# Feed-forward layer over pairs of batches: seven block products in place of eight, with block sums on GpSimd

## The chip, the cores and the metric

The kernel runs on one core of a Trainium2 chip. The core has five engines that run side by side, each with its own queue of instructions in program order: TensorE (PE; its loading of weights is shown apart as PEld), VectorE (DVE), ScalarE (ACT), GpSimd (POOL), and SyncE (SP), which here only issues DMA transfers. The metric is the device time of one execution in microseconds (us). Unchanged, it was 1137.98 us (median of 3 runs, 1137.89 to 1138.92).

## The reference

Attention with a sigmoid in place of the softmax, and then a feed-forward layer with an exact GELU:

```python
scores = (q @ k.T) / np.sqrt(64) - np.log(448)     # 8 batches, 12 heads, 448 positions, 64 wide
x = sigmoid(scores) @ v                            # gathered to 3584 rows of 768
h = x @ w_in                                       # 768 -> 2048
g = 0.5 * h * (1.0 + erf(h / np.sqrt(2.0)))
out = g @ w_out                                    # 2048 -> 768
```

The inputs q, k, v are float32; w_in and w_out are float64.

## The kernel before

**Attention.** A loop over 24 units (a batch and four heads each) runs on PE with sigmoids on ACT. Its output x, laid out with features on partitions, goes to the DRAM scratch `scr_x` from GpSimd's queue. The float64 weights come in as 64-bit integers. `Decoder` turns a chunk of them (16 of 768 columns for w_in, 24 of 512 for w_out) into float32 by five DVE instructions (lines 99 to 124) and two on ACT (110, 113), and GpSimd's queue stores the result in `scr_in` or `scr_out`. 22 of the 40 chunks are decoded beside attention, the other 18 at the start of the feed-forward part (`dec.to`).

**Feed-forward.** `feed_forward` walks over 7 tiles of T = 512 columns of x. In `ffn1` each of the 16 feature blocks of h takes one weight unit and 6 blocks of 128 input features; in `ffn2` each of the 6 output blocks takes two units with 8 blocks of g each. Every product is in split precision: an operand is rounded to a high part (`fp32r`) and the rest is kept as a low part, and three matmuls (low weights by high data, high by low, high by high) are summed in PSUM. So a tile has 16·6·3 + 6·16·3 = 576 matmuls of 512 columns.

**What feeds them.** `Weights.get` keeps three units loaded (`wst`, from scratch by SP, line 173) and four split (`whl`). A split is one cast on ACT for the high part (line 184) and one subtraction on DVE for the low part (line 185). x is loaded and split once for a tile (lines 200 to 207), and g is made by two GELUs on ACT and one subtraction on DVE (413 to 415). Outputs are copied from PSUM by ACT (450) and stored by SP.

**What sets the order.** Each engine runs its instructions in the order in which the code writes them; `ctx.enter_context(tc.manual_schedule())` has no scheduler change it. Buffers rotate, and an instruction that writes a buffer waits for its last reader.

Of the kernel before, what the change touches and what calls it, by code (L numbers as in the profile page):

```python
# [8 lines left out]
F32 = mybir.dt.float32  # L9
# [7 lines left out]
P = 128  # L17
# [4 lines left out]
def tile_sigmoid_attention_gelu_ffn(  # L22
# [19 lines left out]
    T = 512  # L42
    NT = B * S // T
    assert NT * T == B * S and TAIL == D
# [3 lines left out]
    def psum(name, bufs):  # L48
# [7 lines left out]
    xh = const.tile([P, NPAIR, T], F32R, name="xh")  # L56
    xl = const.tile([P, NPAIR, T], F32R, name="xl")

    scr_in = tc.dram_tile([NF, P, NC * P], F32, name="scr_in")
    scr_out = tc.dram_tile([NO, P, NFH * P], F32, name="scr_out")  # L60
    scr_x = tc.dram_tile([P, NPAIR, B * S], F32, name="scr_x")
    WU = max(NC, NFH) * P
    SUB_IN, SUB_OUT = NC * P, NFH * P // 2
    SUB = max(SUB_IN, SUB_OUT)
    WHL, WST = 4, 3
    UNITS = [("in", u) for u in range(NF)] + [("out", u) for u in range(NO)]
    CHUNKS = [
        (kind, u, c0, sub)
        for kind, u in UNITS
        for n, sub in ((NC * P, SUB_IN) if kind == "in" else (NFH * P, SUB_OUT),)  # L70
        for c0 in range(0, n, sub)
    ]

    def width(kind):
        return (NC if kind == "in" else NFH) * P

    def scratch(kind, u):
        return (scr_in if kind == "in" else scr_out)[u]

    class Decoder:  # L80
        def __init__(self):
            self.raws, self.parts, self.done, self.out = {}, {}, 0, None
            self.steps = self.work()
            self.taken = 0

        def load(self, i):
            if i < len(CHUNKS):
                kind, u, c0, w = CHUNKS[i]
                src = (w_in if kind == "in" else w_out)[u].rearrange("p a b -> p (a b)")
                raw = sb.tile([P, 2 * SUB], U32, tag="raw", name=f"raw{i}", bufs=3)[:, : 2 * w]  # L90
# [24 lines left out]
        def end(self, i):  # L115
            kind, u, c0, w = CHUNKS[i]
# [5 lines left out]
            if c0 == 0:  # L122
                self.out = sb.tile([P, WU], F32, tag="wd", name=f"wd_{kind}{u}", bufs=2)
            nc.vector.scalar_tensor_tensor(  # L124
                self.out[:, c0 : c0 + w], m, 2.0**-31, e.bitcast(F32), op0=ALU.mult, op1=ALU.mult
            )
            if c0 + w == width(kind):
                nc.gpsimd.dma_start(scratch(kind, u), self.out[:, : width(kind)])
                self.done += 1

# [20 lines left out]
        def units(self, n):  # L151
# [7 lines left out]
    class Weights:  # L159
# [336 lines left out]
```

## Time and profile before

| | |
|---|---|
| runs | 1137.98 us (1137.89 to 1138.92, n = 3) |
| profiled execution | 1137.48 us, span 1135.7 us |
| attention, on PE | 0 to 255.03 us |
| feed-forward, first to last matmul | 255.03 to 1131.7 us |
| matmuls in the feed-forward part | 4032, of 512 columns each |
| matmuls in attention | 8 of 512 columns to warm up, 1332 of 448 |
| instructions on GpSimd | 56, 52 of them DMA issues |

The span runs from the first instruction to the last; the execution's own time has 1.8 us more around it. The profile page gives the busy time of each engine, the chain of work that ended last, and groups of instructions by line with their mean duration and the idle time ahead of them. The windows give the same by stretches of time, the timeline single instructions. A matmul's shown duration includes its pipeline, so successive ones overlap: their rate is read from the distance of their starts.

### The profile page before, as it was taken

Reading aid. Unit: us, or ns where it says so; the run is one execution under the profiler, and the core shown is the slowest. Engines: PE = TensorE matmul, PEld = TensorE weight load, DVE = VectorE, ACT = ScalarE, POOL = GpSimd, SP = SyncE. Lnnn points to the kernel's source line nnn. Section 1 sums busy time; section 2 is a strip of 40 time slices with the busy share of each in tenths; the row PEclk is TensorE's granted clock in tenths of the full one; section 3 lists DMA queues with packets and bytes.
Section 4 is the critical chain, followed back from the end, with each engine's and each line's share of the span. In section 5 each row is a group of like instructions: output and inputs, shape, how many; then the busy total and the mean of one; then the engine's idle time right before and its main releaser. Section 6 shows DMA issues by size and latency. Waiting matters only on the chain.

```text
span 1135.7 us, 14635 instructions
## 1 busy us (share of the span) xinstructions
PE 1126.3 (99%) x5858; PEld 892.6 (79%) x5858; DVE 536.2 (47%) x646; ACT 544.7 (48%) x749; POOL 37.6 (3%) x56
## 2 busy tenths in 40 slices
PE   9999999999998999999999999999999999999998
PEld 5545555548887888888888888888888888888887
DVE  3777777658987244314433344324432343324420
ACT  5887787776645244324432344324432443334420
POOL 0111111000000000000000000000000000000000
PEclk9999999999999999999999999999999999999999
DMA  9999998868677334433353333533343335433330
GB/s 276 315 308 301 294 301 278 254 220 253 217 267 272 115 108 133 172 93 121 116 172 111 116 106 121 177 113 109 126 167 116 107 111 176 125 102 101 127 121 28
DMA packets 71444, 194.42 MB, mean 171 GB/s; under 512 B 6992, under 2 KB 19920, under 8 KB 71376
## 3 DMA queue, kind: packets, MB, share of 16 engines
q1 hardware_dynamic: 65376, 169.53, 48.0%
q0 software_dynamic: 5696, 23.60, 5.2%
q8 instruction: 46, 0.75, 0.3%
q10 hardware_dynamic: 304, 0.36, 0.1%
q14 instruction: 22, 0.18, 0.0%
HBM read 158.86 MB, written 34.60 MB: 170 GB/s over the span
## 4 chain that ended last, share of the span: by engine, by line
PE 96%; DVE 2%; ACT 1%; issue 0%; ACTq 0%
PE ph L408 13%; PE ph L409 13%; PE ph L410 13%; PE po L436 12%; PE po L438 12%; PE po L437 12%; PE pav L321 10%; PE sc L283 8%; PE sc_t L300 2%; PE pav L334 2%; DVE me L119 1%; DVE whl L185 1%; DVE wd_out L124 0%; ACT me L110 0%; ACT whl L184 0%; PE warm L361 0%
## 5 line engine op out<-in xcount | busy, mean ns | idle before, releaser
L185 DVE TENSOR_TENSOR whl<-wst,whl 128x768 fp32r<-128x768 f32 (+1 forms) x196 | 209.8, 1072 | 285.5 <-ACT whl L184 283.4
L436 PE MATMUL po<-g,whl 128*128 128x512 f32 x672 | 255.5, 380 | 4.0 <-DVE whl L185 4.0
L438 PE MATMUL po<-g,whl 128*128 128x512 f32 x672 | 255.5, 380 | 0.0
L437 PE MATMUL po<-g,whl 128*128 128x512 f32 x672 | 255.3, 380 | 0.0
L408 PE MATMUL ph<-xh,whl 128*128 128x512 f32 x672 | 254.8, 379 | 0.0
L409 PE MATMUL ph<-xl,whl 128*128 128x512 f32 x672 | 254.7, 379 | 0.0
L410 PE MATMUL ph<-xh,whl 128*128 128x512 f32 x672 | 254.7, 379 | 0.0
L184 ACT CAST whl<-wst 128x768 fp32r<-128x768 f32 (+1 forms) x196 | 181.3, 925 | 123.1 <-PE po L438 113.3
L415 DVE TENSOR_TENSOR g<-gf,g 128x512 fp32r<-128x512 f32 x112 | 77.4, 691 | 208.4 <-ACT g L414 208.3
L413 ACT ACTIVATE gf<-ph 128x512 f32<-128x512 f32 x112 | 66.9, 597 | 208.6 <-PE ph L410 183.4
L266 ACT ACTIVATE a<-sc 128x896 f32<-128x896 f32 x144 | 121.8, 920 | 53.4 <-PE sc L283 53.4
L436 PEld LDWEIGHTS po<-g,whl 128*128 128x128 f32 x672 | 127.4, 190 | 22.9 <-DVE whl L185 4.8
L437 PEld LDWEIGHTS po<-g,whl 128*128 128x128 f32 x672 | 127.4, 190 | 18.2
L408 PEld LDWEIGHTS ph<-xh,whl 128*128 128x128 f32 x672 | 127.0, 189 | 18.7 <-DVE whl L185 0.7
L438 PEld LDWEIGHTS po<-g,whl 128*128 128x128 f32 x672 | 127.3, 189 | 18.2
L410 PEld LDWEIGHTS ph<-xh,whl 128*128 128x128 f32 x672 | 127.0, 189 | 18.1
L409 PEld LDWEIGHTS ph<-xl,whl 128*128 128x128 f32 x672 | 127.0, 189 | 18.0
L321 PE MATMUL pav<-a,v 128*64 128x448 f32 x576 | 119.1, 548 | 0.0
L450 ACT COPY ob<-po 128x512 f32<-128x512 f32 x41 | 24.0, 585 | 161.2 <-PE po L438 161.2
L321 PEld LDWEIGHTS pav<-a,v 128*64 128x64 f32 x576 | 37.0, 136 | 68.0 <-issue 63.6
L414 ACT ACTIVATE g<-ph 128x512 fp32r<-128x512 f32 x112 | 66.2, 591 | 0.0
L347 DVE COPY x<-pav 128x448 f32<-128x448 f32 x48 | 29.9, 624 | 62.1 <-PE pav L321 40.4
(43 smaller groups left out, 700.9 us busy)
## 6 DMA issues: line engine op xcount, KB each, us to landing
wst<-scr_in SPq DMA_DIRECT2D x112, 384.0 KB, 3.2
wst<-scr_out SPq DMA_DIRECT2D x84, 512.0 KB, 3.4
v<-v_dram SPq DMA_DIRECT2D x24, 512.0 KB, 5.3
raw<-w_in_dram SPq DMA_DIRECT2D x16, 768.0 KB, 8.3
raw<-w_out_dram SPq DMA_DIRECT2D x24, 512.0 KB, 4.8
scr_x<-x POOLq DMA_DIRECT2D x24, 448.0 KB, 7.0
xl<-scr_x SPq DMA_DIRECT2D x7, 1536.0 KB, 7.8
out_dram<-ob SPq DMA_DIRECT2D x41, 256.0 KB, 2.1
```

The lines of the kernel that those rows point to most:

```text
L184: nc.scalar.copy(hl[:, 0, :w], t[:, :w])
L185: nc.vector.tensor_tensor(hl[:, 1, :w], t[:, :w], hl[:, 0, :w], op=ALU.subtract)
L266: nc.scalar.activation(to, sc, AF.Sigmoid, bias=NEG_LOG_S, scale=SCALE)
L283: nc.tensor.matmul(sc[:, j], ks[rows(j), 1, keys], braid(qs[rows(j), 0]) if braided else qs[rows(j), 0], start=n == 0, stop=n == last,)
L321: nc.tensor.matmul(pav[rows(j)], vals[u][:, p, j, c], a[:, j], start=p == 0 and c == 0, stop=p == 1 and c == FULL - 1,)
L408: nc.tensor.matmul(ph, wl, braid(xh[:, cc]), start=cc == 0, stop=False)
L409: nc.tensor.matmul(ph, wh, braid(xl[:, cc]), start=False, stop=False)
L410: nc.tensor.matmul(ph, wh, braid(xh[:, cc]), start=False, stop=cc == NC - 1)
L415: nc.vector.tensor_tensor(gt[:, 1], gf, gt[:, 0], op=ALU.subtract)
L436: nc.tensor.matmul(po, wl, braid(g[fc][:, 0]), start=fc == 0, stop=False)
L437: nc.tensor.matmul(po, wh, braid(g[fc][:, 1]), start=False, stop=False)
L438: nc.tensor.matmul(po, wh, braid(g[fc][:, 0]), start=False, stop=fc == NF - 1)
```

## The change

**Blocks.** The unit of the feed-forward part is now a pair of batches (4 pairs, b = 0 to 3). Its 896 columns are two blocks (k = 0, 1) of 448, each half of one batch and half of the other. The weights and data are seen as 2 by 2 blocks, and a product of two such matrices is made from seven block products (the Strassen-Winograd scheme) in place of eight. Only the first matrix of the first pair is done plainly (`ffn1_plain`).

**Counts.** The plain one has 16·2·6·3 = 576 matmuls of 448 columns; each of the other seven has 7·72 = 504 (in the first matrix 8 blocks by 3 by 3 terms, in the second 4 steps by 3 by 2 by 3). That is 576 + 7·504 = 4104 matmuls of 448 columns.

**Sums of blocks.** Weights: for each group of four blocks, `mix` makes four sums on GpSimd, and seven DMAs (w_in) or fourteen (w_out) from its queue store the seven operands. For w_out there are 6 groups, formed during `ffn1_plain` as the decoder finishes them; for w_in there are 8, formed in `remix` from the plain scratch `scr_f` during the first pair's second matrix. Data: `x_sum` makes four sums of x on GpSimd for the next pair; `difference_g` (line 501) and lines 672, 674, 675 make sums of g there, 16 of 128x896 for a pair. Results: sums of products stay in PSUM where a chain can be accumulated, else DVE adds them (lines 589 to 595, 652 to 664).

**Splits.** g is kept in float32 and is split when it is used, by `build` (one cast on ACT and one subtraction on DVE of 128x896), two steps ahead, in a ring of three. An operand of x is split by `x_split` (128x1344). A weight unit is 768 wide throughout, 212 of them in place of 196.

```diff
-    T = 512
-    NT = B * S // T
+    NB = B // 2
+    KC, KF, KE = NC // 2, NF // 2, NE // 2
+    IN_ORDER = [
+        (p, s - lag)
+        for chain in ((1, 2), (6, 7, 4), (5, 3))
+        for s in range(KF + len(chain) - 1)
+        for lag, p in enumerate(chain)
+        if 0 <= s - lag < KF
+    ]
+    OUT_ORDER = [(p, c) for p in (1, 2, 5, 6, 3, 7, 4) for c in range(KF // 2)]
...
+    def mix(a, s):
+        a11, a12, a21, a22 = (a[:, i] for i in range(4))
+        s1, s2, s3, s4 = (s[:, i] for i in range(4))
+        nc.gpsimd.tensor_tensor(s1, a21, a22, op=ALU.add)
+        nc.gpsimd.tensor_tensor(s2, s1, a11, op=ALU.subtract)
+        nc.gpsimd.tensor_tensor(s3, a11, a21, op=ALU.subtract)
+        nc.gpsimd.tensor_tensor(s4, a12, s2, op=ALU.subtract)
+        return {1: a11, 2: a12, 3: s4, 4: a22, 5: s1, 6: s2, 7: s3}
...
+        def flush(self):
+            while self.pool and self.pending:
+                (c, e), a = self.pending.pop(0)
+                s = self.pool.tile([P, 4, QUAD], F32, tag="s", name=f"s{c}_{e}", bufs=1)
+                parts = mix(a.rearrange("p (q n) -> p q n", q=4), s)
+                for p in (1, 2, 5, 6, 3, 7, 4):
+                    src = parts[p].rearrange("p (h f n) -> p h f n", h=2, f=2)
+                    for h in range(2):
+                        nc.gpsimd.dma_start(scr_out[p, 2 * c + h][:, :, e], src[:, h])
...
+    def terms(bank, w, op, first, last, chain=False):
+        wh, wl = w
+        hi, lo = op
+        for n, (a, m) in enumerate(((wl, hi), (wh, lo), (wh, hi))):
+            flags = dict(start=first and n == 0, stop=last and n == 2, skip_group_check=chain)
+            nc.tensor.matmul(bank, a, braid(m), **flags)
...
+        def ffn1_plain(g):
...
+            for f in range(NF):
+                if f >= lead:
+                    step(f, 0)
+                step(f, 1)
+                W.prepare_to(f + 1 + WHL)
+                dec.to(AHEAD + 1.5 * (f + 1))
...
+        def ffn1(b, g, ops):
...
+            for n, (p, j) in enumerate(IN_ORDER):
+                if n % 2 == 0:
+                    hl = W.get()
...
+                if (p, j) == (1, 2):
+                    x_split(ops, b, 6)
+                after = {(1, KF - 1): 7, (2, KF - 1): 4, (6, KF - 1): 5, (7, KF - 1): 3}
+                if (p, j) in after:
+                    x_split(ops, b, after[p, j])
...
+            for n, (p, c) in enumerate(OUT_ORDER):
+                hl = W.get()
+                build(n + 2)
...
+                if ahead[0] == 5:
+                    t1, g22 = g[0, 1][ahead[1]], g[1, 1][ahead[1]]
+                    nc.gpsimd.tensor_tensor(t1, g22, t1, op=sub)
+                if p == 6:
+                    nc.gpsimd.tensor_tensor(g11, t2, g11, op=sub)
+                    nc.gpsimd.tensor_tensor(g21, g21, t2, op=sub)
+                if b == 0 and n % 3 == 2 and n // 3 < KF:
+                    remix(n // 3)
...
+        def remix(j):
+            a = sb.tile([P, 4 * QUAD], F32, tag="wd", name=f"a{j}", bufs=2)[:, : 2 * WU]
+            for i in range(2):
+                nc.sync.dma_start(a[:, i * WU : (i + 1) * WU], scr_f[i * KF + j])
+            s = ff.tile([P, 4, QUAD], F32, tag="s", name=f"sin{j}", bufs=1)[:, :, :OP]
+            parts = mix(a.rearrange("p (q n) -> p q n", q=4), s)
+            for p, part in parts.items():
+                n = IN_ORDER.index((p, j))
+                nc.gpsimd.dma_start(scr_in[n // 2][:, n % 2], part)
```

Three places show how the order on an engine changes. The first is PE in the first matrix. Before, in `ffn1`, the rows of one feature block (`ph_6`) are followed by those of the next, each into its own bank, three terms in turn:

```order
L408 MATMUL ph_6_5594<-xh,whl_5508 128x512
L409 MATMUL ph_6_5594<-xl,whl_5508 128x512
L410 MATMUL ph_6_5594<-xh,whl_5508 128x512
L408 MATMUL ph_7_5623<-xh,whl_5537 128x512
L409 MATMUL ph_7_5623<-xl,whl_5537 128x512
L410 MATMUL ph_7_5623<-xh,whl_5537 128x512
```

Now, in the second pair's `ffn1` (`pf` a PSUM bank, `xh_p` and `xl_p` the split operand of a block product), PE alternates between the products of a chain:

```order
L472 MATMUL pf_4819<-xh_p_4757,whl_4777 128x448 x2
L472 MATMUL pf_4819<-xl_p_4758,whl_4777 128x448
L472 MATMUL pf_4819<-xh_p_4757,whl_4777 128x448
L472 MATMUL pf_4875<-xh_p_4721,whl_4777 128x448
L472 MATMUL pf_4875<-xl_p_4722,whl_4777 128x448
L472 MATMUL pf_4875<-xh_p_4721,whl_4777 128x448 x2
```

A matmul has 448 columns for 512, one weight unit serves two products, and a bank is returned to by a second product after others have gone to other banks.

The second place is GpSimd. Before, its queue in the feed-forward part holds only the stores of decoded weights, and it ends with them:

```order
L128 DMA scr_out<-wd_out_3292 128x1024
L128 DMA scr_out<-wd_out_3343 128x1024
L128 DMA scr_out<-wd_out_3398 128x1024
L128 DMA scr_out<-wd_out_3448 128x1024
L492 UNCONDITIONAL_BRANCH
```

Now, in the first pair's second matrix, it holds this (`a` four loaded blocks of w_in, `sin` their sums, `g_01`, `g_11` blocks of g):

```order
L703 DMA scr_in_77<-sin_4123 128x384
L703 DMA scr_in_79<-sin_4123 128x384
L672 TENSOR_TENSOR g_01_3_2772<-g_11_3_2780,g_01_3_2772 128x896
L91 TENSOR_TENSOR sin_4220<-a_4217 128x384
L92 TENSOR_TENSOR sin_4220<-sin_4220,a_4217 128x384
L93 TENSOR_TENSOR sin_4220<-a_4217 128x384
L94 TENSOR_TENSOR sin_4220<-a_4217,sin_4220 128x384
L703 DMA scr_in_70<-a_4217 128x384
L703 DMA scr_in_72<-a_4217 128x384
```

Sums of weights, their stores and sums of g stand in one queue, in the order of the code.

The third place is DVE in the second matrix. Before, in the third tile, there is one subtraction for a weight unit of 1024 and, at the tile's middle, two for x:

```order
L185 TENSOR_TENSOR whl_5169<-wst_5109,whl_5169 128x1024
L207 TENSOR_TENSOR xl<-xl,xh 128x1536 x2
L185 TENSOR_TENSOR whl_5202<-wst_5139,whl_5202 128x1024
L185 TENSOR_TENSOR whl_5235<-wst_5172,whl_5235 128x1024
L185 TENSOR_TENSOR whl_5264<-wst_5205,whl_5264 128x1024
```

Now, in the first pair (`op` the split operand of a step, `tmp` an output, `y` a kept product):

```order
L234 TENSOR_TENSOR whl_4461<-wst_4397,whl_4461 128x768
L263 TENSOR_TENSOR op_21_4466<-g_00_1_2766,op_21_4466 128x896
L660 TENSOR_TENSOR tmp_4475<-pf_4098,y_2_3817 128x448
L660 TENSOR_TENSOR tmp_4484<-pf_4099,y_2_3817 128x448
L660 TENSOR_TENSOR tmp_4493<-pf_4100,y_2_3817 128x448
L234 TENSOR_TENSOR whl_4496<-wst_4438,whl_4496 128x768
L263 TENSOR_TENSOR op_22_4501<-g_00_2_2767,op_22_4501 128x896
```

Each step of 18 matmuls has two subtractions, one for the weights and one for the data, and after a chain's last step the additions that end it.

More of the change, by code (lines that the diff above doesn't have):

```diff
@@ L67, in tile_sigmoid_attention_gelu_ffn @@
[L67 to L71, printed above, removed]
-    ]
[L74 to L78, printed above, removed]
+    WU = NC * P
+    QUAD = KF // 2 * P
+    RAW = 2 * max(WU, 2 * S)
+    WHL, WST = 4, 3
+    IN_ORDER = [
[5 more added lines that the diff above has]
+    ]
@@ new lines, in tile_sigmoid_attention_gelu_ffn @@
+    OUT_ORDER = [(p, c) for p in (1, 2, 5, 6, 3, 7, 4) for c in range(KF // 2)]
+    OP = KC * P
+    assert OP * 2 == WU and KE * P * 2 == WU
+    scr_x = tc.dram_tile([P, NPAIR, B * S], F32, name="scr_x")
+    scr_f = tc.dram_tile([NF, P, WU], F32, name="scr_f")
+    scr_in = [tc.dram_tile([P, 2, OP], F32, name=f"scr_in{i}") for i in range(len(IN_ORDER) // 2)]
+    scr_out = {
+        pc: tc.dram_tile([P, 2, KE, P], F32, name=f"scr_out{pc[0]}_{pc[1]}") for pc in OUT_ORDER
+    }
+    CHUNKS = [("in", u, 0, WU, 0, 0) for u in range(NF)] + [
+        ("out", 2 * ee + h, c * QUAD, QUAD, ij, (c, e))
+        for c in range(2)
+        for e in range(KE)
+        for ij, (ee, h) in enumerate(((e, 0), (e, 1), (e + KE, 0), (e + KE, 1)))
+    ]
@@ L149, in to, with until @@
                 self.taken += 1
-        def units(self, n):
-            while self.done < min(n, len(UNITS)):
+        def until(self, units, groups):
+            while self.done < units or self.groups < groups:
                 next(self.steps)
@@ L244, in load_v, with split_qk @@
             vals[u] = vr
-        def split(u, p):
+        def split_qk(u, p):
             if u >= total:
@@ L374, in attention @@
                 values(u - 1, 0)
[L375 to L376 removed]
+            split_qk(u + 1, 0)
+            split_qk(u + 1, 1)
             for c in range(FULL):
@@ L389, in attention @@
             if u == total - 2:
-                load_x(0)
+                for j in range(2):
+                    x0.append((x_tile("xs", f"xh0_{j}"), x_tile("xs", f"xl0_{j}")))
+                    load_x(x0[j][1], 0, j, 0)
                 W.load_to(2)
             if u == total - 1:
-                split_x()
+                for hi, lo in x0:
+                    split(hi, lo, lo.bitcast(F32))
                 W.prepare_to(2)
```

359 lines of the change are left out of this document (257 added, 102 removed).

## The prediction

> **What bounds the kernel now.** I read the page's busy times first, then windows of the feed-forward part, then the waits. The busy times:
>
> ```profile
> span 1135.7 us, 14635 instructions
> PE 1126.3 (99%) x5858; PEld 892.6 (79%) x5858; DVE 536.2 (47%) x646; ACT 544.7 (48%) x749; POOL 37.6 (3%) x56
> ```
>
> A busy PE is not a PE at its peak, so the rate has to be seen. The windows (length, then busy time and count of PE, PEld, DVE, ACT and POOL, granted clock, DMA share, GB/s) show the start of the feed-forward part, the stretch after it, and the steady one:
>
> ```profile
> 255.00:340.00 85.00, 85.00 (x396) 74.43 (x395) 75.17 (x110) 50.46 (x81) 5.41 (x8) 1.00 0.75 244
> 340.00:400.00 60.00, 56.03 (x251) 48.15 (x250) 32.70 (x40) 24.95 (x34) 1.94 (x3) 0.97 0.57 193
> 400.00:1100.00 700.00, 700.00 (x3245) 612.98 (x3244) 251.26 (x262) 266.22 (x386) 0.00 (x0) 1.00 0.40 126
> ```
>
> In 700 us 3245 matmuls start: 215.7 ns for one of 512 columns, at full clock and without a gap. DVE and ACT are at 36% and 38% there. So in the feed-forward part PE's columns are the bound, except near 340 to 400 us, where PE loses 4.0 us. The waits (who waits for whom, us in total, times, longest) name the cause:
>
> ```profile
> PE po L436 <- DVE whl L185: 4.0, 2, 3.7
> ```
>
> A low part of a weight came late, behind decoding: DVE is busy 75 of the 85 us before.
>
> **What the change removes and adds on PE.** Away go 4032 matmuls: 4032·0.2157 = 869.7 us. In come 4104 of 448 columns. Attention has such matmuls, with half the rows, in pairs on the two halves of the array (PE timeline: start, duration, what, count):
>
> ```profile
> 202.38 0.46 PE L283 MATMUL sc<-lo,hi 64*128 64x448 f32 x2
> 202.68 0.35 PE L283 MATMUL sc<-hi,lo 64*128 64x448 f32 x2
> ...
> 204.00 0.35 PE L283 MATMUL sc<-hi 64*128 64x448 f32 x2
> ```
>
> From 202.68 to 204.00 there are seven starts: 188.6 ns each, which is 215.7·448/512 = 188.7 as well. 4104·0.1886 = 774.0 us. **PE's gain is 95.7 us.** The first row shows what a weight load costs when nothing covers it: 0.30 us to the next start in place of 0.19, so 0.11 us, less than a matmul of 0.19 that runs over it. I therefore take 188.6 ns though each matmul still brings its own load; the load's recorded duration (below, rival 3) is the other end.
>
> The old stall goes: 4.0 us, and the clock of 0.97 over 60 us beside it, 1.8 us. Against the profiled execution (1137.5 us; span 1135.7 and 1.8 around it; the median of the runs, 1138.0, is 0.5 above) a PE that never waits gives 1137.5 − 95.7 − 5.8 = **1036.0 us**. Attention, its decoding and the 8 warming matmuls stay; the tail (a DVE addition in place of ACT's and DVE's copies, and a store) I cost at nothing.
>
> **ACT and DVE.** Their prices, from the groups by shape (count, busy us, mean ns, idle before):
>
> ```profile
> L185 DVE TENSOR_TENSOR whl<-wst,whl 128x768 fp32r<-128x768 f32 x112 | 107.1, 957 | 101.5 <-ACT whl L184 99.4
> L184 ACT CAST whl<-wst 128x768 fp32r<-128x768 f32 x112 | 93.2, 833 | 47.7 <-PE po L438 42.5 <-DMA wst<-scr_in 5.2
> L184 ACT CAST whl<-wst 128x1024 fp32r<-128x1024 f32 x84 | 88.1, 1048 | 75.4 <-PE po L438 70.8 <-DMA wst<-scr_out 4.6
> L258 DVE TENSOR_TENSOR lo<-qk,hi 128x896 fp32r<-128x896 f32 x47 | 51.0, 1085 | 4.3 <-ACT hi L255 2.6 <-DMA v<-v_dram 0.8
> L347 DVE COPY x<-pav 128x448 f32<-128x448 f32 x48 | 29.9, 624 | 62.1 <-PE pav L321 40.4 <-PE pav L334 21.6
> L207 DVE TENSOR_TENSOR xl<-xl,xh 128x1536 fp32r<-128x1536 f32 x14 | 24.0, 1755 | 0.8
> L206 ACT CAST xh<-xl 128x1536 fp32r<-128x1536 f32 x14 | 20.0, 1474 | 0.0
> L255 ACT CAST hi<-qk 128x896 fp32r<-128x896 f32 x21 | 19.9, 950 | 0.0
> L413 ACT ACTIVATE gf<-ph 128x512 f32<-128x512 f32 x112 | 66.9, 597 | 208.6 <-PE ph L410 183.4 <-issue 25.2
> ```
>
> A matrix of seven products takes PE 504·0.1886 = 95.1 us. *Second matrix:* DVE has 28 weight and 28 data subtractions and two of x (1344 wide, 1.56 us by the slope of its rows), 28·(0.957 + 1.085) + 3.1 = 60.3 us, and 15 additions from PSUM of about 0.62, together 70 us. ACT has 28·(0.833 + 0.950) + 2·1.31 + 9·0.54 (a GELU's 0.597 cut to 448) = 57 us. *First matrix:* DVE 28·0.957 + 40·0.62 + 5·1.56 = 59, ACT 23 + 40·0.54 + 5·1.31 = 51. *Plain first matrix* (576·0.1886 = 108.6 us): DVE has 18 chunks of decoding at 3.3 us,
>
> ```profile
> L103 DVE SCALAR_TENSOR_TENSOR me<-raw,me 128x512 uint32<-128x512 uint32 x24 | 19.2, 800 | 0.8
> L119 DVE SCALAR_TENSOR_TENSOR me<-raw,me 128x512 uint32<-128x512 uint32 x24 | 19.1, 797 | 0.2
> L124 DVE SCALAR_TENSOR_TENSOR wd_out<-me 128x512 f32<-128x512 uint32 x24 | 16.6, 692 | 0.8
> L100 DVE TENSOR_SCALAR me<-raw 128x512 uint32<-128x512 uint32 x24 | 11.8, 491 | 0.0
> L99 DVE TENSOR_SCALAR me<-raw 128x512 uint32<-128x512 uint32 x24 | 11.5, 479 | 0.0
> ```
>
> 58.7 us, 16 weight units (15.3) and two of x (3.1): 77 us. All of it fits beside PE if nothing else holds DVE; weights are split three steps ahead (10 us) and data two (6.8 us).
>
> **GpSimd.** No row shows GpSimd computing. Bounds for a sum of two 128x896 blocks: the same work on DVE, 1.09 us; or two passes of an engine that reads one operand at a time, as ACT's cast does, 2·0.950 = 1.90. I take the upper end, because GpSimd's lanes must fetch two operands and the ACT row is the nearest with one operand at a time; both ends stay in the range. By the same doubling 384 wide costs 1.02, 512 wide 1.27, 1344 wide 2.62. GPSIMD Engine Reference of the Trainium skill (3.1, Elementwise, side-by-side cycle accounting) has 4497 ns for a sum of 2048 float32, by proportion an estimated 1.97 us for 896; no run here shows it yet, and the sums below would be some 4% larger. Issues from its queue (timeline) and the time to landing (DMA issues) are there:
>
> ```profile
> 36.57 0.79 POOL L128 DMA_DIRECT2D scr_in<-wd_in  x1 [1.11 <-DVE wd_in L124]
> 188.84 0.71 POOL L350 DMA_DIRECT2D scr_x<-x  x1 [7.62 <-DVE x L347]
> 190.70 0.57 POOL L128 DMA_DIRECT2D scr_in<-wd_in  x1 [1.15 <-DVE wd_in L124]
> wst<-scr_in SPq DMA_DIRECT2D x112, 384.0 KB, 3.2
> scr_in<-wd_in POOLq DMA_DIRECT2D x16, 384.0 KB, 6.8
> ```
>
> At 0.71 for an issue, the plain matrix gives GpSimd 24 sums of 512, 4 of 896 and 84 issues: 38 + 60 = 98 us of 108.6. **The first pair's second matrix** gives it 32 sums of 384, 12 of 896, 4 of 1344 and 56 issues: 33 + 23 + 10 + 40 = 106 us of 95.1. That is too much. Its first remix starts after three steps (10 us); all but the last x sum are ahead of the eighth remix's end, so that ends at 10 + 103 = 113, has landed at 120, is loaded at 123 and split at 125 (0.83 + 0.96). PE wants this data, product (1, 7), 14th of 56 in the next matrix at 1.70 us each: 95.1 + 13·1.70 = 117.2. So 8 us late on GpSimd's own time. A later pair has 23 + 10 = 33 us of sums here, which are hidden.
>
> **Taking turns.** DVE and GpSimd do get in each other's way. The GpSimd issue of 36.57 ended at 37.36, the one of 190.70 at 191.27, while DVE ran
>
> ```profile
> 36.65 0.59 DVE L100 TENSOR_SCALAR me<-raw 128x768 uint32<-128x768 uint32 x1
> 37.27 0.97 DVE L103 SCALAR_TENSOR_TENSOR me<-raw,me 128x768 uint32<-128x768 uint32 x1
> 190.65 0.43 DVE L100 TENSOR_SCALAR me<-raw 128x512 uint32<-128x512 uint32 x1
> ```
>
> The first issue is longer, and ends 0.12 us after DVE's L100; L103, with two operands, then runs over its end. So single-operand DVE work holds an issue up. Whether a GpSimd sum and a two-operand DVE subtraction hold each other up, no row shows: nothing below, a full turn of the other above. I take half a DVE subtraction, met as often as DVE is busy with one: 60.3/95.1 = 0.63, times 0.51 us, times the 47 sums ahead = 15 us, all on the late data. Elsewhere the lead of splits hides most: 2 us for each later second matrix, where eight sums of 896 follow each other (lines 674, 675), 3 for the plain matrix, 2 for the seams. With the 8: 23 + 6 + 3 + 2 = 34 us. **Forecast: 1036.0 + 34 = 1070 us.**
>
> **Rivals.** *1. GpSimd's sums cost nothing to PE*: a sum is priced as on DVE. The second matrix then has 18 + 13 + 6 + 40 = 77 us, done before PE wants it; 1036 plus a few us for seams and tail, 1042. For it speaks that DVE and ACT have 25 to 40 us of slack in every matrix; against it, the price at its lowest.
>
> *2. Full turns*: each GpSimd sum blocks DVE's two-operand work for its whole time and the reverse. In the first pair's second matrix 60 us of DVE and 66 of sums share 95 us; each of 47 sums waits some 0.5 us more, so the data is 33 late in place of 23. In a later one eight sums of 1.9 let one subtraction through each: a step that needs two then takes 2·(1.9 + 1.02) = 5.8 us in place of 3.4 for four steps, and the four sums before them take up the lead: 10 us in each of three. With 6 for the plain matrix, where decoding slows as well, and 2: 71 us, 1107. Page SBUF — State Buffer of the Trainium skill (Who interferes with whom, and the reading of its diagram) states such a lock: exclusive, for the whole instruction, also for DVE with two SBUF inputs against a GpSimd instruction that reads SBUF. The 0.12 us above agrees for issues; the sums are untested here. By that rule the time is this rival's.
>
> *3. The load of weights sets the rate.*
>
> ```profile
> L408 PEld LDWEIGHTS ph<-xh,whl 128*128 128x128 f32 x672 | 127.0, 189 | 18.7 <-DVE whl L185 0.7
> ```
>
> 189 ns is all of a 448-column matmul. If the next could start only some 4 ns after the load's end, 4104·0.004 = 17 us more: 1087. Against it: the 0.11 us above.
>
> *4. Slower than before: GpSimd is the bound of the first pair.* There the time is linear in the price of a sum. Its 104 us of sums and 100 us of issues in the first two matrices already use the time; each tenth on the price is 10 us late at product (1, 7). The 102 us gained are gone when a sum costs 1.75 times my value (over 3.3 us for 896): 34 + 0.75·104 = 112. At twice, 1036 + 34 + 104 = 1174. Nothing in the profile gives such a price.
>
> **How the numbers follow.** Forecast 0.45 (1055 to 1090), rival 1 0.25, rival 2 0.18, rival 3 0.04, rival 4 0.08. The range of 1038 to 1112 leaves out rival 4, and some of the edges of rivals 1 and 2. Faster by over 0.2% (2.3 us, about what a measurement of this kernel can tell from no change) 0.91; within 0.02; slower 0.07.
>
> **What would show it.** Starts of matmuls 188.6 ns apart in a later pair (rival 3: over 192). A wait of PE, through SP's load of `wst`, for a store from GpSimd's queue, in the first 25 us of the second pair's first matrix, some 23 us long (none: rival 1). The mean of GpSimd's 128x896 sums: 1.1 or 1.9 us. In later second matrices PE's waits for DVE at the steps that follow product 5: about 2 us (10: rival 2). I am wrong if PE stalls in first matrices of later pairs, where GpSimd has 8 us of sums.

## The result: 3.4% slower, and the profile after

The changed kernel takes 1177.05 us (median of 4 runs, 1176.37 to 1178.78), the kernel before 1138.10 us in the same comparison (4 runs). The ratio is 1.0343, with a 95% interval of 1.0325 to 1.0361. Forecast were 1070 us, with a range up to 1112.

The page of the changed kernel, with the two lines that answer to those of before:

```profile
span 1175.2 us, 15595 instructions
PE 1071.8 (91%) x5930; PEld 924.2 (79%) x5930; DVE 838.6 (71%) x852; ACT 607.3 (52%) x810; POOL 400.8 (34%) x316
```

PE is no longer busy all the time, though it has less to do. Windows of its eight matrices, from the first matmul of each to that of the next (length, busy time and count of PE, PEld, DVE, ACT and POOL, granted clock, DMA share, GB/s). I call them 1a (the plain first matrix of the first pair), 1b (its second matrix), 2a, 2b and so on to 4b:

```profile
256.07:385.94 129.87, 111.95 (x577) 109.78 (x577) 96.69 (x112) 52.94 (x89) 104.50 (x112) 0.94 0.65 211
385.94:517.62 131.68, 105.85 (x505) 101.43 (x505) 108.84 (x68) 51.12 (x65) 103.10 (x94) 0.87 0.69 239
517.62:628.77 111.15, 99.51 (x505) 97.15 (x505) 69.11 (x80) 51.33 (x76) 23.13 (x17) 0.97 0.41 131
628.77:740.94 112.17, 102.40 (x505) 98.50 (x506) 94.29 (x71) 52.47 (x66) 47.07 (x17) 0.95 0.43 138
740.94:844.79 103.85, 96.24 (x506) 94.83 (x504) 60.29 (x76) 50.72 (x75) 7.09 (x4) 1.00 0.37 117
844.79:959.44 114.65, 104.90 (x505) 100.51 (x505) 94.08 (x71) 52.44 (x66) 47.04 (x17) 0.93 0.42 135
959.44:1063.29 103.85, 96.25 (x506) 94.83 (x504) 60.30 (x76) 50.69 (x75) 7.09 (x4) 1.00 0.37 117
1063.29:1171.00 107.71, 101.17 (x504) 98.07 (x504) 80.39 (x67) 47.63 (x61) 32.95 (x13) 0.95 0.32 101
```

Forecast were 108.6 us for the plain one and 95.1 for the others, plus 34 in all. Each is longer, the two of the first pair most: 21 and 37 us. The last columns show a loss that the forecast did not have at all: the granted clock falls to 0.87 in 1b, and over the span it is 0.961 on average (0.998 before). It is halved in 15 stretches of 92.7 us in all. In 32.6 us of them PE has no matmul and loses nothing by it; in the other 60.1 us it works at half speed. So about 30 us go to the clock.

Two views point at a cause: PE's waits, and the groups of DVE and GpSimd (count, busy us, mean ns, idle before):

```profile
PE pf L472 <- DVE op L263: 49.5, 24, 12.8
PE pf L472 <- ACT op L262: 25.2, 5, 13.9
...
L234 DVE TENSOR_TENSOR whl<-wst,whl 128x768 fp32r<-128x768 f32 x212 | 282.1, 1332 | 182.0 <-ACT whl L233 181.8
L263 DVE TENSOR_TENSOR op<-g,op 128x896 fp32r<-128x896 f32 x112 | 184.5, 1651 | 4.7 <-ACT op L262 4.7
L675 POOL TENSOR_TENSOR g<-g,g 128x896 f32<-128x896 f32 x16 | 43.0, 2688 | 0.0
L674 POOL TENSOR_TENSOR g<-g,g 128x896 f32<-128x896 f32 x16 | 42.5, 2658 | 0.0
L672 POOL TENSOR_TENSOR g<-g,g 128x896 f32<-128x896 f32 x16 | 34.1, 2137 | 97.1 <-DVE op L263 97.0
L595 DVE TENSOR_TENSOR tmp<-pf,g 128x448 f32<-128x448 f32 x72 | 42.4, 616 | 10.3 <-PE pf L472 10.3
```

The same subtraction of 128x768 took 957 ns before and takes 1332 on average here; that of 128x896 went from 1085 to 1651. The addition that reads one operand from PSUM (line 595) is at its expected 0.62 us. The sums of lines 674 and 675, where DVE subtracts all the time, take over 0.5 us more than those of line 672. The timeline (start, duration, and the idle time ahead in brackets) shows it happen, first GpSimd, then DVE, then PE, in 1b:

```profile
458.66 2.10 POOL L674 TENSOR_TENSOR g<-g,g 128x896 f32<-128x896 f32 x1
460.70 2.08 POOL L675 TENSOR_TENSOR g<-g,g 128x896 f32<-128x896 f32 x1
...
468.81 2.06 POOL L675 TENSOR_TENSOR g<-g,g 128x896 f32<-128x896 f32 x1
470.84 1.70 POOL L91 TENSOR_TENSOR sin<-a 128x384 f32<-128x384 f32 x1
...
457.42 14.27 DVE L234 TENSOR_TENSOR whl<-wst,whl 128x768 fp32r<-128x768 f32 x1
471.62 1.88 DVE L263 TENSOR_TENSOR op<-g,op 128x896 fp32r<-128x896 f32 x1
...
473.55 4.75 PE L472 MATMUL pf<-op,whl 128*128 128x448 f32 x15 [12.79 <-DVE op L263]
```

One subtraction lasts 14.27 us: six sums of GpSimd run from 458.66 to 470.87 without a gap, and it ends only when they have. PE then stands for 12.8 us (13.1 from start to start; gaps are given so below). In 2b the two engines alternate instead, and each instruction lasts as long as both together:

```profile
672.73 2.95 POOL L675 TENSOR_TENSOR g<-g,g 128x896 f32<-128x896 f32 x1
675.65 2.80 POOL L674 TENSOR_TENSOR g<-g,g 128x896 f32<-128x896 f32 x1
...
673.64 2.86 DVE L234 TENSOR_TENSOR whl<-wst,whl 128x768 fp32r<-128x768 f32 x1
676.43 2.97 DVE L263 TENSOR_TENSOR op<-g,op 128x896 fp32r<-128x896 f32 x1
```

That suggests, and does not yet show, that the two exclude each other. Three theories were put to the test. **T1**: GpSimd's sums and DVE's subtractions exclude each other, and the stalls cost PE's clock as well. **T2**: GpSimd's own queue takes too long, so data is late. **T3**: the new order has seams of its own (casts behind each other on ACT, splits that are issued late), whatever engine makes the sums.

### The profile page after: what moved, and what is told of

It reads as the page before. It is cut to its first block, busy times and chain, and to the rows that moved or that the text cites. A ratio compares the mean times of both kernels' runs of the same rounds, so it can differ in the third digit from the quotient of the medians.

```text
span 1175.2 us, 15595 instructions
## 1 busy us (share of the span) xinstructions
PE 1071.8 (91%) x5930; PEld 924.2 (79%) x5930; DVE 838.6 (71%) x852; ACT 607.3 (52%) x810; POOL 400.8 (34%) x316
## 5 line engine op out<-in xcount | busy, mean ns | idle before, releaser
L472 PE MATMUL pf<-op,whl 128*128 128x448 f32 x2016 | 415.2, 369 | 76.8 <-DVE op L263 49.5
L472 PEld LDWEIGHTS pf<-op,whl 128*128 128x128 f32 x2016 | 398.0, 199 | 94.0 <-DVE op L263 57.8
L234 DVE TENSOR_TENSOR whl<-wst,whl 128x768 fp32r<-128x768 f32 x212 | 282.1, 1332 | 182.0 <-ACT whl L233 181.8
L233 ACT CAST whl<-wst 128x768 fp32r<-128x768 f32 x212 | 175.9, 830 | 278.8 <-PE pf L472 198.7
L472 PE MATMUL pf<-xh_p,whl 128*128 128x448 f32 x1008 | 277.7, 355 | 11.8 <-DVE tmp L595 7.3
L472 PEld LDWEIGHTS pf<-xh_p,whl 128*128 128x128 f32 x1008 | 192.1, 191 | 15.4 <-issue 6.3
L263 DVE TENSOR_TENSOR op<-g,op 128x896 fp32r<-128x896 f32 x112 | 184.5, 1651 | 4.7 <-ACT op L262 4.7
L472 PE MATMUL pf<-xl_p,whl 128*128 128x448 f32 x504 | 179.1, 355 | 4.0 <-DVE xl_p L263 4.0
L472 PE MATMUL pf<-xh,whl 128*128 128x448 f32 x384 | 106.0, 357 | 4.5 <-DVE whl L234 3.5
L262 ACT CAST op<-g 128x896 fp32r<-128x896 f32 x112 | 104.2, 935 | 4.7 <-POOL g L672 2.4
```

What stands on the lines that cost most here:

```text
L233: nc.scalar.copy(hl[:, 0], t)
L234: nc.vector.tensor_tensor(hl[:, 1], t, hl[:, 0], op=ALU.subtract)
L262: nc.scalar.copy(hi, src)
L263: nc.vector.tensor_tensor(lo, src, hi, op=ALU.subtract)
L472: nc.tensor.matmul(bank, a, braid(m), **flags)
```

## The experiments

The ideal of 1036.0 us from the prediction is the base. The lengths of the matrices (us) in the runs that tell most, each from the first matmul's start to that of the next (for 4b to that of the last one); they are of the profiled execution, the time is the median:

| run | time | 1a | 1b | 2a | 2b | 3a | 3b | 4a | 4b |
|---|---|---|---|---|---|---|---|---|---|
| ideal | 1036.0 | 108.6 | 95.1 | 95.1 | 95.1 | 95.1 | 95.1 | 95.1 | 95.1 |
| changed kernel | 1177.05 | 129.9 | 131.7 | 111.2 | 112.2 | 103.9 | 114.7 | 103.9 | 107.7 |
| e1, sums of 8 columns | 1079.75 | 115.1 | 103.1 | 102.4 | 98.5 | 101.7 | 96.8 | 101.6 | 98.3 |
| e2, memsets | 1078.77 | 112.8 | 105.0 | 103.7 | 98.5 | 101.7 | 96.8 | 101.7 | 96.6 |
| e12, one operand on DVE | 1108.88 | 125.5 | 115.3 | 105.0 | 98.6 | 101.9 | 99.6 | 101.9 | 99.4 |
| e3, all sums on DVE | 1135.28 | 115.5 | 130.3 | 108.0 | 101.3 | 107.0 | 101.3 | 107.0 | 99.5 |
| e4, sums of g and x on DVE | 1128.40 | 123.7 | 118.8 | 108.0 | 101.2 | 107.0 | 101.2 | 106.9 | 99.5 |
| e9, order mended | 1150.60 | 114.7 | 142.3 | 105.3 | 111.7 | 100.6 | 109.3 | 100.6 | 105.7 |
| e11, weights' sums cut | 1155.18 | 116.4 | 118.4 | 111.2 | 114.7 | 103.9 | 114.6 | 103.8 | 107.7 |
| v4 | 1075.64 | 114.7 | 112.2 | 99.1 | 97.4 | 99.1 | 97.4 | 99.1 | 95.7 |

### e1 and e2: sums that hardly run, and sums that only write

e1 cuts every sum to 8 columns (where a sum was stored or read, an unsummed block mostly takes its place), e2 puts two memsets in its place. Line 501 in both:

```diff
-        nc.gpsimd.tensor_tensor(g[0, 1][c], g[0, 1][c], g[0, 0][c], op=sub)
+        nc.gpsimd.tensor_tensor(g[0, 1][c][:, 0, :8], g[0, 1][c][:, 0, :8], g[0, 0][c][:, 0, :8], op=sub)   # e1
+        fill(g[0, 1][c])          # e2: for _ in range(2): nc.gpsimd.memset(t, 0.5)
```

> Every sum on GpSimd (lines 91 to 94, 501, 553, 672, 674, 675) works on 8 columns in place of 384 to 1344, so most of the sums are left out; places, order, waits and the DMA issues stay. Theory T1 (lock: a GpSimd sum and a DVE subtraction with two SBUF operands exclude each other, and the stalls halve the clock) and T2 (GpSimd's own queue makes data late) both want 1040 to 1070 us, with L234 back at 0.96 us of mean and L263 of 128x896 at 1.09 us. T3 (the new order itself: seams between matrices, casts behind each other on ACT, rings) keeps the loss: over 1120 us.

> Every GpSimd sum is replaced by two memsets of the same output, in the same place: GpSimd is busy there and writes SBUF, but reads nothing (the sums are left out; outputs are constants). If GpSimd's reading is what excludes DVE (T1 as the page on SBUF words it), L234 and L263 go back to 0.96 and 1.09 us and the time is under 1085 us even where GpSimd's busy time in the feed-forward part stays over 250 us. If any GpSimd access to SBUF excludes DVE, L234 stays over 1.2 us. If GpSimd's own lateness is the cause (T2), the time follows its busy time: near 1177 us at an equal busy time, 1040 to 1070 us where the memsets are much shorter.

e1 took 1079.75 us (ratio to the kernel before 0.9513, 0.9477 to 0.955), e2 1078.77 (one run). e1 lies between the ranges of its text, 1070 and 1120 us, so neither side has all of the loss: 98 of the 141 us over the ideal are the sums' doing; the other 43 are not, and stay without them (T3, with whatever else the change brings). In e2 GpSimd is busy three quarters as long as in the changed kernel, 305.9 us of the span where it was 400.8; some 126 of each are issues of DMAs. Its groups:

```profile
L99 POOL MEMSET g<- 128x896 f32 x128 | 108.2, 859 | 390.2 <-ACT g L502 295.4 <-DVE op L267 91.1
...
L238 DVE TENSOR_TENSOR whl<-wst,whl 128x768 fp32r<-128x768 f32 x212 | 202.8, 957 | 240.9 <-ACT whl L237 240.7
L267 DVE TENSOR_TENSOR op<-g,op 128x896 fp32r<-128x896 f32 x112 | 121.1, 1085 | 7.3 <-ACT op L266 7.3
```

Two memsets of 859 ns are 1.72 us, not far from a sum's 2.1. Yet DVE's subtractions are at 957 and 1085 ns, to the nanosecond what they were before. **GpSimd that writes does not disturb DVE.** What is left to disturb it is GpSimd's reading.

### e5: GpSimd reads one operand

```diff
-        nc.gpsimd.tensor_tensor(g11, t2, g11, op=sub)
+        nc.gpsimd.tensor_copy(g11, t2)
```

> Every GpSimd sum becomes one copy of one of its inputs (the sums are left out): GpSimd reads one operand where the sum reads two. If reading at all is what shuts out a DVE instruction with two SBUF operands, L234 and L263 stay clearly over 0.96 and 1.09 us and the time is over 1090 us; if it takes a GpSimd instruction with two operands, they are at 0.96 and 1.09 us as with the memsets, and the time is about 1079 us. A copy that is much shorter than a sum (under 1.0 us for 128x896) would make the loss small in both cases; then only the durations decide.

1087.71 us (one run): just below the 1090 expected if reading excludes. The durations decide, as that text says for short copies: copies of 128x896 took 0.94 us at line 670 (672 before the edit), and 1.45 and 1.60 where DVE is busy; L234 took 1050 ns on average, L263 1263. One operand on GpSimd's side is enough to exclude; the copies are only shorter.

### e6, e8, e10, e12: one operand on DVE's side

The low part is computed by an instruction with one SBUF operand. The four runs differ only in how it is read and written:

```diff
-            nc.vector.tensor_tensor(hl[:, 1], t, hl[:, 0], op=ALU.subtract)
+            nc.vector.tensor_scalar(hl[:, 1], hl[:, 0], 0.001, None, op0=ALU.mult)             # e6
+            # e8: operand's two halves interleaved; e10: both in 3 (7) interleaved parts
+            nc.vector.tensor_scalar(*views(hl[:, 1], hl[:, 0]), 0.001, None, op0=ALU.mult)     # e12
...
+    def views(lo, hi):
+        k = 3 if lo.shape[-1] % 3 == 0 else 7
+        lo = lo.rearrange("p (c b a) -> p c b a", c=k, a=2)
+        return lo, hi.rearrange("p (c a b) -> p c b a", c=k, a=2)
```

> GpSimd's sums are as in the changed kernel, but the low part of every split (lines 234 and 263) is made by DVE from one SBUF operand (high part times 0.001; the true low part is left out). T1: no lock, so GpSimd's sums run in their own time in every stage (about 2.1 us for 128x896, no more 2.7), PE loses only what GpSimd's own queue costs: 1080 to 1110 us, with what is lost over the 1079 of the memsets in the first pair's two matrices. If the loss came from GpSimd's own lateness (T2), 1150 us or more.

> As the run before with one SBUF operand on DVE (the true low part is left out), but the operand is read with a stride (columns j and j + half in turn), so that DVE works at one element a cycle: L234 near 0.9 to 1.0 us and not the 0.56 seen there. GpSimd's sums are those of the changed kernel. Lock only for two SBUF operands or the doubled rate (T1): the longest L234 falls from 14.3 us to under 2 us, GpSimd's 128x896 sums take about 2.1 us in every stage, and the second matrices of the later pairs fall to 97 to 101 us; what stays over 1079 us is GpSimd's own time in the first pair: 1085 to 1110 us. If one DVE operand from SBUF is shut out as well, L234's mean stays over 1.2 us and the time over 1140 us.

> Again one SBUF operand for the low part on DVE (the true low part is left out), read and written in three (768 wide) or seven (896 and 448 wide) interleaved parts, an odd number, since the odd view of x in the last such run is the one that took 1.59 us and not 0.86: L234 near 0.95 us, L263 of 896 near 1.1 us, the same DVE time as a true subtraction. GpSimd's sums are those of the changed kernel. If two SBUF operands on DVE (or its doubled rate) are what excludes GpSimd, both engines now run freely: the longest L234 is under 2 us, line 674 and 675's sums are 2.1 us, later second matrices 97 to 101 us, and the whole 1090 to 1115 us, the rest over 1079 being GpSimd's own time in the first pair (and the decoder's two-operand instructions there). If DVE's time alone matters and not its operands: as the changed kernel, 1160 to 1180 us.

> As the last run with one operand (the true low part is left out), but the operand is read in 3 (7) pieces of two interleaved halves each and written in one piece, as in the one case so far that took 1.59 us for 1344 and not 0.86; so L234 should take 0.9 to 1.0 us undisturbed, and L263 of 896 about 1.1. If one SBUF operand at one element a cycle is shut out like two, L234 and L263 still run in turns with the sums (medians beside sums of 2.5 us and more) and the time is 1150 to 1180 us; then the number of operands is not what matters. If it is not shut out, the longest L234 is under 2 us, the sums of line 674 take 2.1 us, and the time is 1085 to 1115 us; then the run before had a form in which DVE takes both paths at a lower speed.

The first three, one run each, missed what they were to test. In e6 (1117.94 us) and e8 (1127.70) the median of L234 was 0.56 and 0.57 us: 1.4 elements a nanosecond, where the subtraction does 0.8. And its longest instruction still took 14.26 and 14.00 us, behind the same sums; in e6:

```profile
447.61 14.26 DVE L234 TENSOR_SCALAR whl<-whl 128x768 fp32r<-128x768 f32 x1 [0.69 <-ACT whl L233]
```

In e10 (1166.02) the shortest was 0.84 us, and the two engines alternated as in 2b above. So a single operand can be shut out too. e10 lies in the range that its text gave to the other reading, 1160 to 1180 us: on it alone one would say that the operands do not matter.

e12 took a form known from e8 to go at the subtraction's rate (1.59 us for 1344), and came out at 1108.88 us (one run). Its groups, then its timeline in 1b, GpSimd and DVE:

```profile
L684 POOL TENSOR_TENSOR g<-g,g 128x896 f32<-128x896 f32 x16 | 33.5, 2096 | 0.0
L239 DVE TENSOR_SCALAR whl<-whl 128x768 fp32r<-128x768 f32 x212 | 206.1, 973 | 240.8 <-ACT whl L238 240.8
L273 DVE TENSOR_SCALAR op<-op 128x896 fp32r<-128x896 f32 x112 | 122.9, 1102 | 17.5 <-ACT op L267 17.5
```

```profile
453.67 2.10 POOL L685 TENSOR_TENSOR g<-g,g 128x896 f32<-128x896 f32 x1
455.73 2.10 POOL L684 TENSOR_TENSOR g<-g,g 128x896 f32<-128x896 f32 x1
457.80 2.09 POOL L685 TENSOR_TENSOR g<-g,g 128x896 f32<-128x896 f32 x1
459.85 1.00 POOL L91 TENSOR_TENSOR sin<-a 128x384 f32<-128x384 f32 x1
...
453.75 0.98 DVE L239 TENSOR_SCALAR whl<-whl 128x768 fp32r<-128x768 f32 x1 [1.41 <-ACT whl L238]
454.71 1.11 DVE L273 TENSOR_SCALAR op<-op 128x896 fp32r<-128x896 f32 x1
```

The same sums in the same places, DVE instructions slightly longer than the subtractions, and neither engine sees the other: no L239 is over 1.0 us, and the sums take 2.1. This settles T1: **a GpSimd instruction that reads SBUF and a DVE instruction with two SBUF operands, or with one in a faster form, exclude each other.** The Trainium skill, SBUF — State Buffer, "Who interferes with whom", states this rule: DVE has a way of its own for one operand and shares a second one with GpSimd, locked for a whole instruction, also in the modes that use both ways for one operand. e2, e5, e6 and e12 agree with it. It also puts e10 in its place, if its form was such a mode; no run shows that.

In time: 1177.05 − 1108.88 = **68 us for the exclusion**, of which 15 are clock (half of the 60.1 us of matmuls at half clock in the changed kernel, less half of 30.0 in e12). And 1108.88 − 1078.77 = **30 us for GpSimd's own time (T2)**, 23 of them in 1a and 1b. The decoder's two-operand instructions in 1a are still shut out in e12, so a part of its 13 us there belongs to T1. e12 and e2 were run once each, and four runs of one kernel here lie up to 8 us apart, so the two numbers are good to some us.

### e3 and e4: sums on DVE

> All sums move to VectorE, in the same places of the program; GpSimd keeps its DMA issues only. The result is complete. T1: the DVE prices go back to 0.96 and 1.09 us; DVE gets some 0.54 us for each 384 sum, 0.67 for 512, 1.09 for 896 and 1.6 for 1344; in the first pair's second matrix 70 + 17 + 13 + 6 = 106 us of DVE stand against 95 of PE, elsewhere DVE has room: 1060 to 1100 us. T2 and T3: with T2 alone as much, with T3 over 1120 us. Telling T1 from T2: T1 wants the 16 us excess of the second pair's first matrix and the 9 to 20 us of later second matrices to fall below 8 us each; T2 wants only the first pair's matrices and the second pair's first matrix to gain.

> Only the sums of g and x (lines 501, 553, 672, 674, 675) move to VectorE; the sums of weights (lines 91 to 94) stay on GpSimd. The result is complete. T1: later second matrices lose their excess above 8 us (they had 17, 20 and 13), the first pair keeps most of its 58 us, less where line 672 to 675 starved L234: 1110 to 1145 us. T2: GpSimd has 19 + 24 us less to do in the first pair's second matrix, so product (1, 7) of the next matrix is on time, and only there is a gain: 1150 to 1165 us.

e3 took 1135.28 us (0.9975, 0.9964 to 0.9985), e4 1128.40 (0.9923, 0.9907 to 0.9939). In both, the second matrices of the later pairs fell from 112, 115 and 108 to 101, 101 and 100 us as T1 wants. e4 came within T1's range of 1110 to 1145, far from T2's. e3 missed T1's 1060 to 1100 and lies where its text put T3, over 1120: the later first matrices gained only 3 us or lost 3, and 1b stayed at 130. In 1b DVE, whose instructions run in order, stands for a load (its waits in 1b):

```profile
DVE sin L91 <- DMA a<-scr_f: 27.9, 7, 7.0
```

What stood ahead of the sum on GpSimd's queue at no cost now held up the splits behind it. A sum cannot be moved without its wait.

### e7: are back-to-back sums the trouble?

```diff
                 if p == 6:
                     nc.gpsimd.tensor_tensor(g11, t2, g11, op=sub)
-                    nc.gpsimd.tensor_tensor(g21, g21, t2, op=sub)
+                if 17 <= n <= 20:
+                    g21, t2 = g[1, 0][n - 17], g[0, 1][n - 17]
+                    nc.gpsimd.tensor_tensor(g21, g21, t2, op=sub)
```

> Line 675's four sums for each pair (g21) go from the steps of product 6, where they follow line 674's, to four later steps of their own (the 18th to 21st), so that no two sums of g stand in one step. The result is complete. If back-to-back sums are what starves DVE (its subtraction gets no turn between them), the gap of 13 us in the first pair's second matrix and the 9 to 20 us excess of the later ones go: 10 to 20 us less in the first, 5 to 10 in each later, 1140 to 1155 us. If each sum costs PE the same wherever it stands (only turns, one subtraction held up by one sum), 1170 to 1180 us.

1174.57 us (1.0329, 1.0312 to 1.0347): no. The longest gap in 1b fell from 13.1 to 8.0 us, and others came for it; 2b and 3b took 112.8 and 113.2. For these four sums of each pair, waiting one's turn costs about the same at either place.

### e9 and e11: the order, and the two kinds of sums

e9 keeps all sums on GpSimd and mends the order: the first two splits of a second matrix (`build`) are issued ahead of the last steps of the first one, line 501 three steps later, and the operands of products 7 and 3 are split in three pieces.

> The changed kernel with only the order mended as in v1 (first two splits of a second matrix issued earlier, line 501 three steps later, operands of products 7 and 3 split in three pieces); all sums stay on GpSimd. The result is complete. If the lock carries most of the loss: 8 to 10 us less for each first matrix of a later pair with its seam, little in the first pair: 1140 to 1160 us. If the order was the main loss and the lock only made it visible: 1095 to 1125 us.

> The changed kernel with the sums of weights (lines 91 to 94) cut to 8 columns, so most of those sums are left out; the sums of g and x stay on GpSimd. If the loss is the shared time of DVE's two-operand instructions and GpSimd's sums, the plain first matrix takes 113 to 117 us (it was 130), the first pair's second one becomes like the second pair's, 108 to 115 us (it was 132), and the rest stays: 1135 to 1150 us. If the sums of g and x did nothing in the first pair, its second matrix falls to 103 as without any sums: 1125 to 1135.

e9 took 1150.60 us (1.0115, 1.0101 to 1.013), within the range of T1, but not by its parts: 26 us less in all, with 15 won in 1a, where little was expected, and 3 to 6 in each later first matrix, where 8 to 10 were, while 1b loses 11. Mending the order does not save the change. e11 took 1155.18 (one run), 5 over the upper end: 1a came out as expected at 116, 1b 3 over. So the sums of weights cost 22 us, and those of g and x 75 (1155.18 to e1's 1079.75).

### v1 to v4: a version that beats both

All four have the mended order and the sums of g, x and w_out on DVE. v1 keeps the w_in sums on GpSimd; v2 moves two of their eight groups into 1a; v3 is v2 with their blocks loaded from GpSimd's queue; v4 makes them on DVE, with the load two steps ahead of the sum:

```diff
-                if b == 0 and n % 3 == 2 and n // 3 < KF:
-                    remix(n // 3)
+                if b == 0 and n % 3 == 1 and n // 3 < KF:
+                    mixing = fetch(n // 3)
+                if b == 0 and n % 3 == 0 and n > 0 and n // 3 <= KF:
+                    remix(n // 3 - 1, mixing)
```

> A version with a complete result: the sums of g, of x and of w_out on DVE, those of w_in on GpSimd; the first two splits of a second matrix are issued ahead of the last steps of the first one; the difference of g (line 501) is issued three steps later; the operands of products 7 and 3 are split in three pieces. From the runs so far: first matrix of the first pair 115 (sums of w_out on DVE) less 3 for its seam, its second matrix 119, then for each later pair 108 less 4 (seam) less 4 (late splits) less 4 (the wait for line 595) and 101: 1098 to 1112 us. If the seams are not what the moved splits cover, 1118 to 1124.

> As v1, with two of the eight sums of w_in blocks (remix 0 and 1) issued in the last three feature blocks of the plain first matrix, and the six others every fourth step of the first pair's second matrix in place of eight every third. The result is complete. Taking DVE's instructions with two SBUF operands and GpSimd's sums as one server, that matrix has 79 + 24 times 1.5 = 115 us where v1 had 79 + 32 times 1.5 = 127 (it took 115 for a matrix of 95): 8 to 12 us less, 1066 to 1071 us. If what v1 loses there is not the shared server but single waits for DVE: 1075 to 1079.

> v2 with the loads of the blocks of w_in (line 698's) issued from GpSimd's queue and not from SP's, where in v2 they waited 14.6 us for a buffer with the loads of weights for PE behind them. The result is complete. If that wait is what made v2 slower than v1, the first pair's second matrix falls from 122 to 105 to 112 us: 1066 to 1076 us. If it is GpSimd's sums beside DVE, as v1 or v2: 1078 to 1086.

> v1 with the sums of w_in on DVE too (so none is left on GpSimd, and nothing takes turns), their blocks loaded two steps ahead of the sums, so that DVE's queue does not stand at the load as it did when all sums were simply moved to DVE. The result is complete. DVE has 106 us in the first pair's second matrix (it took 115 in v1, 130 with all sums on DVE in place): 106 to 112 us there, 1069 to 1076 in all. If DVE's queue still stands at other waits: 1080 to 1095.

| version | us (4 runs) | ratio to before, 95% |
|---|---|---|
| v1 | 1078.38 (1077.33 to 1080.31) | 0.9482 (0.9468 to 0.9496) |
| v2 | 1086.15 (1083.37 to 1087.37) | 0.9544 (0.9528 to 0.9559) |
| v3 | 1095.50 (1092.37 to 1100.57) | 0.9646 (0.9621 to 0.9671) |
| v4 | 1075.64 (1073.86 to 1077.83) | 0.9445 (0.9428 to 0.9462) |

v1 was 20 us better than expected, and v4 came where it should. v2 and v3 missed, each by a wait in another queue. In v2, SP's loads of the blocks stood in front of the weights (SP's queue, 366 to 400 us):

```profile
SPq L714 <- DMA scr_in<-a: 9.6, 2, 7.5
SPq L714 <- DMA scr_out<-wd: 5.0, 1, 5.0
```

v3 freed SP, and 1b fell from 122.4 to 112.7 us; but GpSimd now had the loads too, the sums came late, and 2a rose from 99.1 to 116.9, with a cast on ACT that waited for them (ACT's waits there):

```profile
ACT whl L233 <- DMA wst<-scr_in: 21.9, 3, 12.1
```

The page of v4 has the same two lines as above:

```profile
span 1076.1 us, 15565 instructions
PE 1044.4 (97%) x5930; PEld 908.3 (84%) x5930; DVE 781.6 (73%) x996; ACT 608.1 (57%) x822; POOL 119.6 (11%) x184
```

DVE has all the sums and is busy 57 us less than in the changed kernel, where it had none of them. v4 takes 8.6% less than the changed kernel. Of the 40 us that are left over the ideal, 1b has 17.

## Why the prediction was wrong

Point by point, by its own steps:

- **PE's gain (95.7 us) and the rate** were right. In v4's last matrix the last of 504 matmuls starts 95.67 us after the first, 190.2 ns from one to the next with its few gaps. Rival 3 (over 192) is out.
- **The price of a sum** was nearly right: undisturbed, 2.10 us for 128x896 (taken: 1.90), 1.00 for 384 (1.02), 1.26 for 512 (1.27), 3.05 for 1344 (2.62).
- **"Taking turns" is the step that failed.** It held a turn to cost half a DVE subtraction, paid by GpSimd: 15 us, with 6 for the later second matrices and a part of 3 for the plain one. Measured: 68. The text had no row for it, and it chose a value between its two ends that priced only one of the two engines. The other side is dearer: each sum keeps DVE from subtracting for its own 2.1 us, and DVE is what PE waits for. The seams (below) were missed by nearly as much, 41 us; either miss alone would have taken the forecast to about the range's end, 1112.
- **Rival 2 had the mechanism**, and was given 0.18. Its 1107 fell short by 70. It counted late data and the 10 us of a later second matrix, which is of the right size (97 to 100 us in e2 and e12, 112, 115 and 108 here); its sign, 10 us of PE's waits for DVE behind product 5 where the forecast had 2, came as 7.8 us in 2b and in 3b. But it left 1b itself at 95 us, though it had put 60 us of DVE and 66 of sums into it: one after the other 126, and 131.7 were measured, with seams and the clock among them. And it took the seams and the clock from the forecast.
- **GpSimd's own time** (8 us, late at product (1, 7)) was 30, and at another place. No wait of 23 us came early in 2a: 1b, longer by 37, gave its sums the time. The largest loss is at the seam from 1a to 1b. The text allowed 3 us for the plain matrix and 2 for all seams, since 98 us of work fit into 108.6. But the last group of w_out can be summed only when the last chunk is decoded, at 371 us, as the matrix ends (GpSimd's timeline, then ACT's):

```profile
371.24 1.90 POOL L91 TENSOR_TENSOR s<-wd 128x512 f32<-128x512 f32 x1 [2.83 <-DVE wd L143]
379.13 6.24 POOL L166 DMA_DIRECT2D scr_out<-s  x8
...
382.61 0.83 ACT L233 CAST whl<-wst 128x768 fp32r<-128x768 f32 x1 [11.31 <-DMA wst<-scr_out]
```

  PE stood 14.3 us there; 2.5 in e2 and in e11. In e11, whose sums of weights have 8 columns, the last group is summed at 364 us, 8 before the matrix ends.
- **Seams (2 us)**: what stays without any sum is 43, the most for a single small term: in e2, 7 to 9 us for each later first matrix, 2 to 3 for each later second one, 4 and 10 for 1a and 1b. PE's waits make 31 of it, at the seams and inside the matrices, 10 of them for the casts of `op` on ACT. The order is a part: in v4, where it is mended, later first matrices take 99.1 us in place of 101.7. No run has the mended order and no sums, so how much of the rest is order stays open.
- **The clock** was in no term. The prediction removed the old stall with the clock beside it, and gave its own new stalls none: about 30 us, which are contained in the three measured terms.
- "I am wrong if PE stalls in first matrices of later pairs": it did. 3a and 4a were each 8.8 us over the ideal, 6.6 of which stay without any sums.
- Rival 4 gave 1174 us, next to the result, for another reason: it wanted sums of over 3.3 us. They appeared to take 2.7, and PE waited for DVE most of the time; GpSimd's own time made 30 of the 141 us.

So 1036.0 + 43 (what stays without sums) + 30 (GpSimd's time) + 68 (exclusion) = 1177. The terms are differences between runs, so that they add up proves nothing; the durations of the single instructions in e2 and e12 carry them.

## What to carry to other kernels

Work that is moved to an engine with slack must be checked for what it shares with the engine that PE waits for. Add up the busy times of those two in each stage, as if they were one: 126 us for a stage of 95 shows the loss before any run. It is a warning and not a price: in 2b the same sum (60 us of DVE's subtractions, 37 of GpSimd's sums at their undisturbed prices) is some 97, and 112 were measured. When such a price is unknown and its ends are far apart, price both engines' waits, and let the cheap experiment (the same work, writing only) come before the choice. A seam between stages is a latency, from the last input to the first use, and is not hidden by room in the sums; and a stall can bring a lower clock after it, to be counted with it: here about a third again of the waits.

## What the runs showed of the hardware, not expected

- A DVE instruction that finds GpSimd reading can wait through six sums in a row (14.27 us for 0.96 us of work), and at another place the two alternate strictly. What decides between them stays open. In the records the long one begins 1.24 us before the first of the six, while GpSimd issues stores, so which of the two began first does not decide it; beside the same issues in e2 no such subtraction takes over 0.96 us. In e7 PE's longest wait for a subtraction of `op` was 6.9 us in place of 12.8, and the time only 2.5 us less.
- The clock halves soon after a stall begins, and stays so for some us. Windows of the changed kernel around the 6.95 us gap at 427.1 and the 13.1 us gap at 460.4:

```profile
425.00:429.20 4.20, 2.28 (x11) 1.66 (x9) 2.96 (x1) 1.67 (x2) 4.18 (x4) 0.99 1.06 400
429.20:439.40 10.20, 5.36 (x14) 4.87 (x15) 10.20 (x6) 4.41 (x6) 8.13 (x6) 0.50 0.86 304
...
463.20:477.00 13.80, 3.45 (x9) 3.15 (x10) 13.80 (x5) 0.00 (x0) 13.72 (x8) 0.51 0.31 104
```

  In the last window PE has matmuls for 3.45 of 13.8 us, so most of that slow stretch fell into the stall itself and cost nothing. All waits of PE in the feed-forward part add up to some 96 us and the clock's loss to about 30, so a stall cost about a third again as much as it lasted. In the records the slow stretches last 3.4 us or multiples of it. Short gaps bring one or not: in e2 one matmul starts 2.7 us after the one before it, and the next 1.1 us after that, alike at three seams. At the first seam 11 matmuls start in the 3.4 us after it, at the second 20 (windows of the seam and of the time after it, twice):

```profile
574.00:579.30 5.30, 2.25 (x11) 1.62 (x10) 3.81 (x5) 3.81 (x6) 2.19 (x3) 1.00 0.24 79
579.30:582.70 3.40, 3.40 (x11) 3.06 (x10) 2.15 (x3) 0.56 (x1) 0.00 (x0) 0.50 0.34 86
774.20:779.50 5.30, 2.25 (x11) 1.63 (x11) 3.81 (x5) 3.82 (x6) 2.15 (x3) 1.00 0.24 76
779.50:782.90 3.40, 3.40 (x20) 3.40 (x19) 2.13 (x3) 1.07 (x2) 0.00 (x0) 1.00 0.33 98
```

  The Trainium skill, TensorE: Matmul & The Clock Gate, "Why this matters for your kernels", warns of idle times over some 3 us between bursts; here 2.7 and 1.1 from start to start, with one matmul between them, were enough in one case of three.
